# Splitting the second FFN product's matmuls into 256 columns, and another order of SBUF tiles

## The chip, the cores and the metric

The kernel runs on one NeuronCore of one Trainium2 chip. The metric is the device time of one execution in microseconds (us), from outside the program; the profile's span, from the first to the last instruction, is a few us shorter.

## The reference

Linear attention over 8 batches, 8 heads, 576 positions and a head dimension of 64, followed by a feed-forward network (FFN) on 4608 tokens of 512 values with 2048 hidden units, all in float32:

```python
q_s = softmax(q, axis=-1)
k_s = softmax(k, axis=2)
kv  = einsum('bhsd,bhse->bhde', k_s, v)
x   = einsum('bhsd,bhde->bhse', q_s, kv)     # 4608 tokens x 512 after reshaping
h   = x @ w_in                               # first FFN product, 512 -> 2048
g   = h * sigmoid(1.702 * h)
out = g @ w_out                              # second FFN product, 2048 -> 512
```

## The kernel before, in words

The 4608 tokens are taken in nine tiles of 512 (`t` from 0 to 8). For each tile the hidden units are taken in eight steps (`NS`) of two blocks of 128. All values of both products are split into a high and a low part of type float32r, and each product is the sum of three: high by high, high by low, low by high (the loop over `e`).

In tiles 0 and 1 the first product is `plain1` (L794): matmuls of 512 columns, stationary operand a tile `wj`, moving operand a tile `xp`. In tiles 2 to 8 it is `ffn1` (L841): seven smaller products in each step, from which the hidden values are added up on VectorE. Each of the seven is six matmuls of 256 columns; the stationary operand is a 128-column slice of `wj` or `wt` (two buffers of each kind, taken in turn by the step's parity), the moving operand half a row of a tile `xo`. So there are 7 x 8 x 7 = 392 such products, 2352 matmuls.

The second product is `ffn2` (L904), in all nine tiles: eight units in each step, each unit three matmuls of 512 columns into one of four PSUM banks. The stationary operand is a 128-column slice of `gh` or `gl` (the activation's high and low part), the moving operand a row of a tile `w` (half of the weight's high and low part). That is 9 x 8 x 8 = 576 units, 1728 matmuls. Every MATMUL of the program comes with a LDWEIGHTS of its own, also where two that follow each other have the same stationary operand.

Between these, for the next tile, the attention runs: products of k and v (L634), transposes of q (L683), and q times kv (L704).

The order of the work on every engine is made by the class `Plan` on the host, before anything runs: each operation is given an engine, a cost and a rank, and `Plan.forward` makes an order from them. The ranks of TensorE's operations lay L841's products and L904's units side by side through a step (L892 and L760).

The tiles in SBUF are allocated one behind the other by `sb`, in the order in which the program names them (L196 to L251, and later ones as they are first used). In one partition a tile of `gs`, `wj`, `xo` or `w` takes 4096 bytes, one of `wt` 8192, a `g`, `kt`, `qt`, `qT` or `tmp` 2048, all of them multiples of 512. Those that aren't: four `vt` and `vl` of 2080 bytes (4 x 512 + 32), two `qm` and `r` of 32, and `first` of 64 (L251), which stands behind all `wj`, `wide` and `wt0` and ahead of the tiles for `w`, `xp` and `xo`. `wt1` is first used, and so allocated, behind `first`; `gs` stands ahead of `vt`, `qm`, `r` and `vl`. Slices begin at multiples of 512 bytes of their tile. So where the operands of a matmul begin, modulo 512 bytes, follows from this order:

| line | stationary | moving | moving less stationary, modulo 512, before |
|---|---|---|---|
| L841 | `wj`, `wt0` | `xo` | 64 |
| L841 | `wt1` | `xo` | 0 |
| L794 | `wj` | `xp` | 64 |
| L904 | `gh`, `gl` | `w` | 4 x 32 + 32 + 2 x 32 + 32 + 64 = 320 |

Of the kernel before, what the change touches and what calls it, by code (L numbers as in the profile page):

```python
# [10 lines left out]
F32R = mybir.dt.float32r  # L11
# [125 lines left out]
def efficient_attention_then_gelu_ffn(  # L137
# [27 lines left out]
    nc = tc.nc  # L165
    B, H, S, D = q.shape
    NTOK, DM = out.shape
    FF = w_out.shape[0]
    P = 128
    C = 4  # L170
    TB = P * C
    HT = TB // 2
    NB = NTOK // TB
    NP = H // 2
# [4 lines left out]
    CM = SM // P  # L179
    ST = S - SM  # L180
    W = D + 1
# [9 lines left out]
    bank = [psum.tile([P, 512], F32, name=f"bank{i}") for i in range(8)]  # L191

    def sb(name, shape, dtype=F32, tag=None):
        return const.tile(shape, dtype, name=name, tag=tag or name)

    ident = sb("ident", [P, P])  # L196
    kvn = [sb(f"kvn{i}", [P, NP, D]) for i in range(2)]
    gt = [[sb(f"g{i}{u}", [P, 2, HT]) for i in range(2 - u)] for u in range(2)]
    gs = [[sb(f"g{s}{i}", [P, 2, 2, HT], F32R) for i in range(2)] for s in "hl"]
    tt = sb("tt", [P, 4, HT])  # L200
    tmp = [sb(f"tmp{i}", [P, DM]) for i in range(2)]
    kt = [sb(f"kt{i}", [P, 2, CM, D]) for i in range(NP)]
    vt = [sb(f"vt{i}", [P, 2, CM, W]) for i in range(NP)]
    qt = [sb(f"qt{i}", [P, C, 2, D]) for i in range(NP)]
    qT = [sb(f"qT{i}", [P, TB]) for i in range(2)]
    mx = [sb(f"mx{i}", [P, 2, D]) for i in range(NP)]
    m1 = sb("m1", [P, 2, 2, D])
    qm = [sb(f"qm{i}", [P, 2 * C]) for i in range(2)]
    r_ = sb("r", [P, 2, NP])
    rs = [r_[:, i] for i in range(2)]  # L210
    kl, vl = sb("kl", [P, H, D]), sb("vl", [P, H, W])
    wj = [[sb(f"wj{i}{jj}", [P, 2, KC, P], F32R) for jj in range(2)] for i in range(2)]
    wts = {}

# [4 lines left out]


    wide = sb("wide", [P, 4, DM], tag="wt0")
    kept = [[dram.tile([P, 2 * DM], F32, name=f"kept{p}{jj}") for jj in range(2)] for p in range(NS)]
    kept_t = [dram.tile([P, 4 * DM], F32, name=f"kept_t{p}") for p in range(NS)]

# [75 lines left out]
    def R(t, step, off=0.0):  # L300
        return SLOTS * (NS * t + step) + off
# [42 lines left out]
    def next_tmp(n):  # L344
        nt[n] += 1
        i = nt[n] % n
        return (tmp[i] if i < 2 else wide[:, i - 2]), ("tmp", i)
# [36 lines left out]
    def pair(t, step):  # L384


        return NS - 1 - step if t % 2 else step
# [501 lines left out]
    def ffn2(t, step):  # L889
        p, gi = pair(t, step), step % 2  # L890
        ov = out[t * TB : (t + 1) * TB, :].rearrange("(p c) m -> p c m", c=C)
        slots = iter((2, 2.3, 2.6, 6.3, 6.6, 10.3, 10.6, 13))  # L892
        units = [(c, jj) for jj in range(2) for c in range(C)] if t < 2 else [(c, jj) for c in (2, 3, 0, 1) for jj in range(2)]
        opened = set()
        for c, jj in units:
            u, cs = c // 2, slice(c % 2 * P, (c % 2 + 1) * P)
            first_, last = step == 0 and c not in opened, step == NS - 1 and c in opened
            opened.add(c)

            def run(c=c, jj=jj, u=u, cs=cs, first_=first_, last=last):  # L900
                gx, gl = (gs[e][gi][:, jj, u, cs] for e in range(2))
                wh, wl = wo[p, jj][:, 0], wo[p, jj][:, 1]
                for e, (l, r) in enumerate(((gx, wh), (gx, wl), (gl, wh))):
                    nc.tensor.matmul(bank[c], l, r, start=first_ and e == 0, stop=last and e == 2)  # L904

            rank = R(t, step + 1, next(slots))
            reads = (("gs", gi, 0, u, jj), ("gs", gi, 1, u, jj), f"wo{p}{jj}")
            plan.add("PE", 0.70, reads, (("bank", c),), rank, run)
            if not last:
                continue  # L910
            o, T = next_tmp(2)

            def run_o(c=c, o=o):
                (nc.vector.tensor_copy if c % 2 else nc.scalar.copy)(o, bank[c])

            def run_d(c=c, o=o):
                nc.sync.dma_start(out=ov[:, c, :], in_=o)

            plan.add("DVE" if c % 2 else "ACT", 0.65, (("bank", c),), (T,), rank - PRIOR, run_o)
            plan.add("SP", 0.4, (T,), (("out", t, c),), rank - PRIOR, run_d, size=P * DM * 4)  # L920
# [83 lines left out]
```

## Time and profile before

| | |
|---|---|
| time, median of 3 runs | 853.64 us (851.61 to 854.23) |
| span of the profiled execution | 850.0 us (no other time of it is shown) |
| TensorE busy | 840.8 us, 99% of the span |
| weight loads busy | 720.9 us, 85% |
| VectorE, ScalarE busy | 520.6 us (61%), 496.4 us (58%) |
| mean granted TensorE clock | 0.999 of full speed |

Matmuls are pipelined: the profile gives each a duration from its start to its modelled end, and the next one starts before that. So the busy time of a line is not the time that it costs; this is read from the timeline, as the distance of one group's start from the next one's. In the timeline, adjacent instructions of one line and the same tiles are one row: its start, its length from the first start to the last end, and how many they are.

### The profile page before, as it was taken

What the parts mean: (1) busy time and instruction counts of PE and PEld (TensorE: products, weight loads), DVE (VectorE), ACT (ScalarE), POOL (GpSimd) and SP (SyncE); (2) the same over time, 40 slices, a digit from 0 to 9 for tenths busy, and PEclk for the clock granted to TensorE, in tenths of its full rate; (3) what the DMA queues carried; (4) which work ended last, traced back from release to release, by engine and by line L of the source; (5) the groups of instructions that cost most, each with busy time, mean ns of one, the idle gap of its engine ahead of it and who ended that gap; (6) DMA issues with size and microseconds to landing.
All of it is one profiled execution on the core that took longest, in us unless ns stands there. A gap on an engine that the chain in (4) does not pass through costs nothing.

```text
span 850.0 us, 14608 instructions
## 1 busy us (share of the span) xinstructions
PE 840.8 (99%) x5644; PEld 720.9 (85%) x5644; DVE 520.6 (61%) x1082; ACT 496.4 (58%) x839; POOL 116.5 (14%) x175
## 2 busy tenths in 40 slices
PE   9999999999999999999999999999999999999998
PEld 4686788878898898889988999899988998899996
DVE  8899995989636884456645674475356533353333
ACT  4698879769636757446744766565366533343332
POOL 1000021120114131110211021100110011101110
PEclk9999999999999999999999999999999999999999
DMA  9999945894469738564765385623664165416541
GB/s 290 267 346 359 253 156 173 246 329 159 115 206 250 212 77 235 170 199 106 217 187 160 118 209 189 192 88 98 197 171 155 51 202 171 149 42 207 173 149 51
DMA packets 127845, 155.63 MB, mean 183 GB/s; under 512 B 76576, under 2 KB 105760, under 8 KB 121376
## 3 DMA queue, kind: packets, MB, share of 16 engines
q0 software_dynamic: 25248, 83.37, 32.3%
q1 hardware_dynamic: 102528, 71.32, 28.5%
q8 instruction: 45, 0.74, 0.4%
q14 instruction: 24, 0.20, 0.1%
HBM read 128.45 MB, written 26.21 MB: 182 GB/s over the span
## 4 chain that ended last, share of the span: by engine, by line
PE 93%; DVE 3%; DMA 2%; ACT 1%; issue 1%; DVEq 0%
PE bank L904 44%; PE bank L841 33%; PE bank L794 8%; PE bank L634 2%; PE bank L704 2%; DMA raw<-in_moe_w_out 2%; PE bank L683 2%; PE bank L296 1%; PE bank L582 0%; DVE wj L368 0%; PE bank L583 0%; DVE w L368 0%; DVE raw L337 0%; DVE kt L556 0%; DMA out<-tmp 0%
## 5 line engine op out<-in xcount | busy, mean ns | idle before, releaser
L904 PE MATMUL bank<-w,gh 128*128 128x512 f32 x1152 | 358.6, 392 | 0.3 <-DVE w L368 0.3
L904 PE MATMUL bank<-w,gl 128*128 128x512 f32 x576 | 226.4, 393 | 0.0
L904 PEld LDWEIGHTS bank<-w,gh 128*128 128x128 f32 x1152 | 199.9, 188 | 30.5 <-DVE w L368 1.1
L841 PE MATMUL bank<-xo,wt 128*128 128x256 f32 x1344 | 188.8, 281 | 0.0
L841 PEld LDWEIGHTS bank<-xo,wt 128*128 128x128 f32 x1344 | 177.4, 188 | 11.1 <-DVE g L854 0.8
L841 PEld LDWEIGHTS bank<-xo,wj 128*128 128x128 f32 x1008 | 136.0, 188 | 12.3 <-issue 1.6
L841 PE MATMUL bank<-xo,wj 128*128 128x256 f32 x1008 | 144.6, 279 | 0.5 <-ACT tt L865 0.5
L857 ACT ACTIVATE g<-g 128x512 f32<-128x512 f32 x112 | 58.8, 525 | 143.7 <-DVE g L854 143.1
L904 PEld LDWEIGHTS bank<-w,gl 128*128 128x128 f32 x576 | 108.3, 188 | 23.3
L854 DVE TENSOR_TENSOR g<-bank,tt 128x256 f32<-128x256 f32 x168 | 70.8, 422 | 88.7 <-PE bank L841 88.4
L885 DVE TENSOR_TENSOR gl<-g,gh 128x512 fp32r<-128x512 f32 x112 | 77.3, 691 | 72.3 <-ACT gh L882 71.7
L854 DVE TENSOR_TENSOR tt<-bank,tt 128x256 f32<-128x256 f32 x112 | 47.3, 423 | 105.4 <-PE bank L841 88.2
L397 POOL DMA_DIRECT2D wj<-kept x96 | 59.6, 621 | 378.8 <-PE bank L841 320.2
L794 PE MATMUL bank<-xp,wj 128*128 128x512 f32 x384 | 100.7, 396 | 2.4 <-ACT g L809 1.5
L794 PEld LDWEIGHTS bank<-xp,wj 128*128 128x128 f32 x384 | 71.0, 188 | 21.9 <-issue 2.6
L882 ACT CAST gh<-g 128x512 fp32r<-128x512 f32 x112 | 69.5, 621 | 3.2
L857 ACT ACTIVATE g<-bank 128x256 f32<-128x256 f32 x56 | 21.7, 387 | 73.0 <-PE bank L841 72.8
L545 POOL PARTITION_ALL_REDUCE mx<-mx x32 | 34.6, 1082 | 198.8 <-DVE mx L541 198.7
L397 POOL DMA_DIRECT2D wt<-kept_t x42 | 22.4, 532 | 125.0 <-PE bank L841 125.0
L857 ACT ACT_TABLE_LOAD x27 | 34.6, 1283 | 0.5
L664 ACT ACT_TABLE_LOAD x26 | 33.4, 1283 | 0.5
L865 ACT COPY tt<-bank 128x256 f32<-128x256 f32 x56 | 20.8, 371 | 18.3 <-PE bank L841 18.0
(103 smaller groups left out, 794.9 us busy)
## 6 DMA issues: line engine op xcount, KB each, us to landing
wt<-kept_t POOLq DMA_DIRECT2D x42, 1024.0 KB, 5.3
wj<-kept POOLq DMA_DIRECT2D x54, 512.0 KB, 3.7
wj<-kept POOLq DMA_DIRECT2D x42, 256.0 KB, 4.8
out<-tmp SPq DMA_DIRECT2D x36, 256.0 KB, 3.1
kt<-in_k SPq DMA_DIRECT2D x32, 256.0 KB, 4.5
raw<-in_moe_w_in SPq DMA_DIRECT2D x16, 512.0 KB, 8.5
raw<-in_moe_w_out SPq DMA_DIRECT2D x16, 512.0 KB, 7.4
kept<-wj SPq DMA_DIRECT2D x16, 512.0 KB, 6.9
```

Of the source, the lines that this page charges most:

```text
L397: "POOL", 1.0, (key,), (ring,), R(t, step - 2, off), lambda: nc.gpsimd.dma_start(out=out(), in_=src), size=size
L545: nc.gpsimd.partition_all_reduce(flat, flat, P, bass_isa.ReduceOp.max)
L634: nc.tensor.matmul(pk[r0 : r0 + D, m, cols], lhs, rhs, start=c == 0, stop=c == CM, tile_position=(0, r0))
L664: nc.scalar.activation(x, x, AF.Exp)
L794: nc.tensor.matmul(bank[bk], w[:, l, c, :], x[:, r], start=c == 0 and e == 0, stop=c == KC - 1 and e == 2)
L841: nc.tensor.matmul(ph[bk], w, x[:, r, c, :], start=opens and c == 0 and e == 0, stop=c == 1 and e == 2, skip_group_check=True,)
L854: return lambda: nc.vector.tensor_tensor(out=o, in0=ph[bk], in1=x, op=ALU.add)
L857: return lambda: nc.scalar.activation(o, x, AF.Gelu_apprx_sigmoid)
L865: vec("ACT", act(n), (ZB,), (A,), 2, lambda: nc.scalar.copy(a, ph[Z]))
L882: vec("ACT", act(2 * n), half, H, slot, lambda c=c, gh=gh: nc.scalar.copy(gh, c))
L885: nc.vector.tensor_tensor(out=gl, in0=c, in1=gh.bitcast(F32), op=ALU.subtract)
L904: nc.tensor.matmul(bank[c], l, r, start=first_ and e == 0, stop=last and e == 2)
```

## The change

Each matmul of L904 becomes two (L908 in the new file), one for each half of the 512 columns, with the same stationary operand. And the tiles are named in another order: `vt`, `qm`, `r` and `vl` come ahead of `gs`, and `wt1` is allocated at once behind `wide`, ahead of `first`.

```diff
     kvn = [sb(f"kvn{i}", [P, NP, D]) for i in range(2)]
+    vt = [sb(f"vt{i}", [P, 2, CM, W]) for i in range(NP)]
+    qm = [sb(f"qm{i}", [P, 2 * C]) for i in range(2)]
+    r_ = sb("r", [P, 2, NP])
+    rs = [r_[:, i] for i in range(2)]
+    vl = sb("vl", [P, H, W])
+    gs = [[sb(f"g{s}{i}", [P, 2, 2, HT], F32R) for i in range(2)] for s in "hl"]
     gt = [[sb(f"g{i}{u}", [P, 2, HT]) for i in range(2 - u)] for u in range(2)]
-    gs = [[sb(f"g{s}{i}", [P, 2, 2, HT], F32R) for i in range(2)] for s in "hl"]
...
-    vt = [sb(f"vt{i}", [P, 2, CM, W]) for i in range(NP)]
...
-    qm = [sb(f"qm{i}", [P, 2 * C]) for i in range(2)]
-    r_ = sb("r", [P, 2, NP])
-    rs = [r_[:, i] for i in range(2)]
-    kl, vl = sb("kl", [P, H, D]), sb("vl", [P, H, W])
+    kl = sb("kl", [P, H, D])
...
     wide = sb("wide", [P, 4, DM], tag="wt0")
+    wts[1] = sb("wt1", [P, 2, 4, 2 * P], F32R, tag="wt1")
...
                 for e, (l, r) in enumerate(((gx, wh), (gx, wl), (gl, wh))):
-                    nc.tensor.matmul(bank[c], l, r, start=first_ and e == 0, stop=last and e == 2)
+                    for h in range(2):
+                        cols = slice(h * HT, (h + 1) * HT)
+                        nc.tensor.matmul(
+                            bank[c][:, cols], l, r[:, cols], start=first_ and e == h == 0,
+                            stop=last and e == 2 and h == 1, skip_group_check=True,
+                        )
```

What is left between the stationary and the moving operand's tiles is `first` alone: 64 bytes modulo 512 for L904, and for every product of L841, those with `wt1` among them.

TensorE, a step of a tile from 2 on (`gh`, `gl` with `w` is the second product, `xo` with `wt` or `wj` the first; `ident` with `qt` is a transpose of q), before:

```order
L841 MATMUL bank_68<-xo_2032,wt_1534 128x256 x6
L683 MATMUL bank_69<-ident,qt_94 128x128 x4
L841 MATMUL bank_67<-xo_2046,wt_1534 128x256 x6
L904 MATMUL bank_63<-w,gh_78 128x512 x2
L904 MATMUL bank_63<-w,gl_80 128x512
L904 MATMUL bank_64<-w,gh_78 128x512 x2
L904 MATMUL bank_64<-w,gl_80 128x512
L841 MATMUL bank_68<-xo_2065,wj_109 128x256 x6
```

and now:

```order
L843 MATMUL bank_68<-xo_2386,wt_1765 128x256 x6
L685 MATMUL bank_69<-ident,qt_98 128x128 x4
L843 MATMUL bank_67<-xo_2406,wt_1765 128x256 x6
L908 MATMUL bank_63<-w,gh_83 128x256 x4
L908 MATMUL bank_63<-w,gl_85 128x256 x2
L908 MATMUL bank_64<-w,gh_83 128x256 x4
L908 MATMUL bank_64<-w,gl_85 128x256 x2
L843 MATMUL bank_68<-xo_2428,wj_109 128x256 x6
```

Nothing changes places; the second product's matmuls are twice as many and half as wide, and from tile 2 on no matmul of 512 columns is left in a step but for those of the attention.

TensorE, a step of tile 0 (`xp` with `wj` is the first product there), before:

```order
L904 MATMUL bank_65<-w,gh_77 128x512 x2
L904 MATMUL bank_65<-w,gl_79 128x512
L794 MATMUL bank_68<-xp_458,wj_111 128x512 x3
L904 MATMUL bank_66<-w,gh_77 128x512 x2
L904 MATMUL bank_66<-w,gl_79 128x512
L794 MATMUL bank_68<-xp_464,wj_111 128x512 x3
```

and now:

```order
L908 MATMUL bank_65<-w,gh_82 128x256 x4
L908 MATMUL bank_65<-w,gl_84 128x256 x2
L796 MATMUL bank_68<-xp_459,wj_111 128x512 x3
L908 MATMUL bank_66<-w,gh_82 128x256 x4
L908 MATMUL bank_66<-w,gl_84 128x256 x2
L796 MATMUL bank_68<-xp_465,wj_111 128x512 x3
```

Here too the places are the same, and the first product keeps its 512 columns. On VectorE, ScalarE, GpSimd and SyncE every instruction stands where it stood.

## Rows read from the trace of the kernel before

**Rows 1.** The page: busy time by engine, granted clock by slice, the chain by line.

```profile
PE 840.8 (99%) x5644; PEld 720.9 (85%) x5644; DVE 520.6 (61%) x1082; ACT 496.4 (58%) x839; POOL 116.5 (14%) x175
...
PEclk9999999999999999999999999999999999999999
...
PE bank L904 44%; PE bank L841 33%; PE bank L794 8%; PE bank L634 2%; PE bank L704 2%; DMA raw<-in_moe_w_out 2%; PE bank L683 2%; PE bank L296 1%; PE bank L582 0%; DVE wj L368 0%; PE bank L583 0%; DVE w L368 0%; DVE raw L337 0%; DVE kt L556 0%; DMA out<-tmp 0%
```

**Rows 2.** Groups of instructions by line, whole span: busy us, mean ns, idle before.

```profile
L904 PE MATMUL bank<-w,gh 128*128 128x512 f32 x1152 | 358.6, 392 | 0.3 <-DVE w L368 0.3
L904 PE MATMUL bank<-w,gl 128*128 128x512 f32 x576 | 226.4, 393 | 0.0
L904 PEld LDWEIGHTS bank<-w,gh 128*128 128x128 f32 x1152 | 199.9, 188 | 30.5 <-DVE w L368 1.1
L841 PE MATMUL bank<-xo,wt 128*128 128x256 f32 x1344 | 188.8, 281 | 0.0
L841 PEld LDWEIGHTS bank<-xo,wt 128*128 128x128 f32 x1344 | 177.4, 188 | 11.1 <-DVE g L854 0.8 <-DVE mx L540 0.5 <-issue 0.5
```

**Rows 3.** Timeline of PE, 503 to 513.5 us: start, length, line, tiles, count.

```profile
503.54 0.60 PE L683 MATMUL bank<-ident,qt 128*128 128x128 f32 x4
503.89 0.95 PE L841 MATMUL bank<-xo,wj 128*128 128x256 f32 x6
504.68 0.63 PE L904 MATMUL bank<-w,gh 128*128 128x512 f32 x2
...
506.75 0.84 PE L841 MATMUL bank<-xo,wj 128*128 128x256 f32 x6
507.43 0.84 PE L841 MATMUL bank<-xo,wt 128*128 128x256 f32 x6
508.11 0.62 PE L904 MATMUL bank<-w,gh 128*128 128x512 f32 x2
...
508.80 0.62 PE L904 MATMUL bank<-w,gh 128*128 128x512 f32 x2
...
509.49 1.52 PE L841 MATMUL bank<-xo,wt 128*128 128x256 f32 x12
```

**Rows 4.** Timeline of PE, 513.5 to 525 us, where `wt` is `wt1`.

```profile
514.30 0.87 PE L841 MATMUL bank<-xo,wj 128*128 128x256 f32 x6
515.01 0.63 PE L904 MATMUL bank<-w,gh 128*128 128x512 f32 x2
...
517.77 0.87 PE L841 MATMUL bank<-xo,wj 128*128 128x256 f32 x6
518.48 0.89 PE L841 MATMUL bank<-xo,wt 128*128 128x256 f32 x6
...
520.59 1.60 PE L841 MATMUL bank<-xo,wt 128*128 128x256 f32 x12
522.03 0.63 PE L904 MATMUL bank<-w,gh 128*128 128x512 f32 x2
...
522.73 0.84 PE L841 MATMUL bank<-xo,wj 128*128 128x256 f32 x6
523.41 0.62 PE L904 MATMUL bank<-w,gh 128*128 128x512 f32 x2
```

**Rows 5.** Timeline of PE, 345.9 to 349 us: a product behind L704.

```profile
345.62 0.61 PE L704 MATMUL bank<-qT,kvn 64*64 64x256 f32 x8
346.16 0.95 PE L841 MATMUL bank<-xo,wj 128*128 128x256 f32 x6
346.95 0.62 PE L904 MATMUL bank<-w,gh 128*128 128x512 f32 x2
```

**Rows 6.** Timeline of PE, 728 to 735 us: products behind the last L704.

```profile
728.29 1.09 PE L704 MATMUL bank<-qT,kvn 64*64 64x512 f32 x8
729.31 0.98 PE L841 MATMUL bank<-xo,wj 128*128 128x256 f32 x6
730.12 0.87 PE L841 MATMUL bank<-xo,wt 128*128 128x256 f32 x6
730.83 0.63 PE L904 MATMUL bank<-w,gh 128*128 128x512 f32 x2
```

## The prediction

> **What bounds the kernel now.** I read the page first. TensorE is busy for 99% of the span, the others for 61% at most, the granted clock stands at its upper level, 2.4 GHz, in all forty slices, and of the chain that ended last 44% lies on L904 and 33% on L841 [rows 1]. TensorE waits for nearly nothing: ahead of these lines' matmuls stand 0.3 us of idle time, and ahead of their loads some 30 us that lie under running matmuls [rows 2]. So only the distance from one matmul's start to the next one's counts. The groups by line don't tell it: they give durations that overlap (392 ns for 512 columns, 281 for 256) [rows 2]. The timeline does: a group's start less the one before it.
>
> I count in **blocks** of 1536 columns: one product of L841 (six matmuls of 256) or one unit of L904 (three of 512). Both have to stream the same columns, so by columns alone a block would cost the same in each. It doesn't:
>
> - **Tight**, L841 at 64 bytes apart: 506.75, 507.43, 508.11, 0.68 us each, a row of length 0.84; a row of two blocks 1.52 [rows 3].
> - **Loose**, the same shape at the same 64 bytes: 514.30 to 515.01 and 517.77 to 518.48, 0.71 us each, length 0.87 [rows 4].
> - `wt1`, 0 bytes apart: 520.59 to 522.03, two blocks in 1.44 us, 0.72 each [rows 4].
> - L904, 512 columns, 320 bytes apart: 508.11, 508.80, 509.49, 0.69 each [rows 3]; four units from 515.01 to 517.77, 2.76 us, 0.69 each [rows 4].
>
> Means over all such starts from 226 us to the end, without those around a stop, give the third digit: 0.680 tight, 0.707 loose, 0.718 for `wt1`, 0.689 for L904. Of the 280 products of L841 at 64 bytes 169 are tight and 111 loose; none of the 112 with `wt1` is tight. The timeline's lengths sort them: 0.84 and 1.52 against 0.86 to 0.89 and 1.58 to 1.60, and 0.95 to 0.98 where the first matmul pays a stop.
>
> **What decides between tight and loose** is the point of this change, since afterwards both products run on matmuls of 256 columns at 64 bytes. Three things are to be seen.
>
> 1. A product right behind other work starts loose. Behind the transposes at 503.54 the product costs 0.79 (0.95 long: the stop and then loose ones) [rows 3]; behind the L704 of 728.29 it is 0.98 long and the next product, 0.71, still loose [rows 6]. Of 20 products at 64 bytes right behind L683, L704 or L634, 19 are loose. One is tight: 0.95 long behind an L704, with the six in 0.79 though its stop was longer than that behind transposes [rows 5].
> 2. The pace holds as long as only such products follow. In all 72 places where two or three products at 64 bytes stand right behind one another the second has the pace of the first, as at 506.75 and 507.43 [rows 3] and at 729.31 and 730.12 [rows 6].
> 3. What ends the loose pace are the 512-column units of L904, and now and then `wt1`: loose at 503.89, three units from 504.68 on, tight at 506.75 [rows 3]; loose `wt1` at 520.59, two units, tight at 522.73 [rows 4]. Not always: 514.30 loose, four units, 517.77 loose again [rows 4].
>
> My reading: with 256 columns a weight load is due in each matmul's time, and a load that is a little late stays late; a matmul of 512 has the slack to catch up. The change takes these matmuls out of tiles 2 to 8.
>
> **A rule against the rows.** The rows show one shape at one address distance at two speeds, and a third at 0 bytes [rows 3, 4]. The Trainium skill, in TensorE: Matmul & The Clock Gate, section "Step-by-step: what each phase is for", says that TensorE has two independent read ports and that "Loading the next tile's weights doesn't steal SBUF read bandwidth from the running matmul"; by that the new order of tiles would be worth nothing, part 4 below would be 0 and the sum 1.2 higher. The trace disagrees: 0.718 against 0.680 for the same columns.
>
> **The change, part by part**, in us of the profiled span.
>
> 1. L904 in tiles 2 to 8: 7 x 8 x 8 = 448 units, now six matmuls of 256. If loose 448 x (0.707 - 0.689) = +8.1; if tight 448 x (0.680 - 0.689) = -4.0. I take loose, by points 1 and 2.
> 2. L841's tight products, 169, lose what made them tight: 169 x 0.027 = +4.6; if the pace is tight, 0.
> 3. L841's loose products at 64 bytes, 111: 0; if tight -111 x 0.027 = -3.0.
> 4. `wt1`, from 0 to 64 bytes, 112 products: 112 x (0.707 - 0.718) = -1.2; if tight 112 x (0.680 - 0.718) = -4.3.
> 5. L904 in tiles 0 and 1, 128 units: between 128 x -0.009 = -1.2 and 128 x 0.018 = +2.3. There L794 keeps its 512 columns between the units and can end the loose pace. I take 0.
> 6. One restart in 20 was tight, and such a stretch then stays so until the next stop. I take 8% of the 840 blocks of parts 1 to 4 as tight: 840 x 0.08 x -0.027 = -1.8.
> 7. The 1728 further weight loads of 188 ns [rows 2] cost nothing by themselves: they lie under the matmul ahead of them, as L841 shows, which loads for every 256 columns already and is tight at that. If this cover is thin, it shows as the loose pace, which is priced.
> 8. The moved tiles cost the other engines nothing: no instruction of theirs moves, and they are idle for 39% or more [rows 1]. Nothing waits longer on TensorE, and none of its operations changes places.
>
> Sum: 8.1 + 4.6 - 1.2 + 0 - 1.8 = **+9.7 us**, a span of 859.7. The median of the runs, 853.64, stands 3.6 above the span of the profiled execution, so I predict **863.3 us**. All loose, with tiles 0 and 1: 8.1 + 4.6 - 1.2 + 2.3 = +13.8, 867.4.
>
> **The rivals.**
>
> *The tight pace holds.* Nothing disturbs the alignment that L841 has when it is tight: a stretch that once got into 0.680 stays there, as in the 50 pairs of tight products, and if the restarts land tight the whole of both products runs at it. Sum: -4.0 + 0 - 3.0 - 4.3 - 1.2 = -12.5, 841.1 us. For it: one tight restart exists [rows 5], what decides there is a few ns, and the tiles of q and of its transposes move as well. Against it: 19 of 20. The point from which it decides: about half of the blocks tight, where 11.5 us of loss in parts 1 to 4 become a gain of 11.3. Chance 0.20.
>
> *The mixture stays.* Some other event resets the pace as the 512 columns did, say a weight load that waits for its semaphore, and six in ten blocks are tight as now: a block costs 0.6 x 0.680 + 0.4 x 0.707 = 0.691, so L904 +0.9, `wt1` 112 x -0.027 = -3.0, together -2.1, 851.5 us. For it: the loads of L841 often carry waits. Against it: such waits stand in the 72 places of point 2 too, and none changed the pace there. Chance 0.10.
>
> *A constant for each matmul, and no effect of addresses.* Then a split costs 1728 times that constant. The rows speak against any cost at all: two tight matmuls of 256 take less than one of 512 (0.680 against 0.689 for the block) [rows 3]. Chance 0.03. By the Trainium skill's section "Back-to-back issue gap" of TensorE: Matmul & The Clock Gate the distance is N/2.4 + 2.5 ns; an estimate from that is 1728 x 2.5 ns = +4.3 us, 857.9.
>
> *The change doesn't do what it says*: the order of TensorE shows the split, and the sizes of the tiles give the 64 bytes; I give this no chance of its own.
>
> **How the numbers follow.** A measurement of this kernel tells a difference of about 0.3%, 2.6 us, from none. The loose pace (forecast) has 0.67, spread from 857 to 867 by how many restarts land tight; with the constant per matmul 0.70 are slower. The mixture, 0.10, lies within 0.3%. The tight pace, 0.20, is faster. The likeliest case's own range is 857 to 868. The range that should hold 8 in 10 takes in the mixture and half-tight outcomes at its lower end, and leaves out the clearly tight case: 849 to 868.
>
> **What would show it.** Right: in the timeline from 226 us on, rows of L843 at 0.87 and of L908 (six matmuls: x4 and x2) about 0.71 apart, from one stop to the next, whole stretches at one pace; the stretch from the last L704 to the end (121 us before) longer by 2 us or more; no more idle time ahead of the matmuls. Wrong: rows of 0.84 through whole stretches (the tight rival), or changes from 0.87 to 0.84 within a stretch that has only matmuls of 256 columns (the mixture). Steps 4 and 7 are wrong if products with `wt1` stay at 0.72, or if blocks of either line cost more than 0.72.

## The result, and the profile after

| | before | after |
|---|---|---|
| time, median of 5 runs each | 852.35 us (850.90 to 854.23) | 863.89 us (862.76 to 866.31) |
| span of the profiled execution | 850.0 us | 860.9 us |
| TensorE busy | 840.8 us | 852.9 us |
| weight loads busy | 720.9 us | 807.4 us |
| ratio after to before | | 1.0143, 95% interval 1.0126 to 1.0161 |

The changed kernel is slower by 11.5 us. The page after, with its busy time, the granted clock and the chain by line, where [rows 1] stood:

```profile
PE 852.9 (99%) x7372; PEld 807.4 (94%) x7372; DVE 522.1 (61%) x1082; ACT 496.9 (58%) x839; POOL 116.2 (14%) x175
...
PEclk9999999999999999999999999999999999999999
...
PE bank L908 45%; PE bank L843 32%; PE bank L796 8%; DMA raw<-in_moe_w_out 3%; PE bank L636 2%; PE bank L706 2%; PE bank L685 2%; PE bank L298 1%; PE bank L584 0%; PE bank L585 0%; DVE w L370 0%; DMA out<-tmp 0%; DVE wide L335 0%; DVE wj L370 0%; DVE raw L339 0%
```

TensorE still is the bound, busy for the same share, at the same granted clock, with 1728 more matmuls. The other engines' busy times are those of before within 1.5 us. The groups by line, where [rows 2] stood:

```profile
L908 PE MATMUL bank<-w,gh 128*128 128x256 f32 x2304 | 364.6, 279 | 0.5 <-DVE w L370 0.4
L908 PE MATMUL bank<-w,gl 128*128 128x256 f32 x1152 | 227.9, 279 | 0.0
L908 PEld LDWEIGHTS bank<-w,gh 128*128 128x128 f32 x2304 | 315.0, 188 | 6.2 <-DVE w L370 0.9
```

No new idle time ahead of the matmuls (0.5 us against 0.3), and loads of the same 188 ns. The idle time ahead of the loads that belong to `gh` fell from 30.5 us to 6.2, with a load for every 256 columns now. So again the distance of the starts has to say it. The timeline of PE after, around the same transposes as in [rows 3]:

```profile
507.49 0.60 PE L685 MATMUL bank<-ident,qt 128*128 128x128 f32 x4
507.84 0.95 PE L843 MATMUL bank<-xo,wj 128*128 128x256 f32 x6
508.63 0.63 PE L908 MATMUL bank<-w,gh 128*128 128x256 f32 x4
...
509.34 0.63 PE L908 MATMUL bank<-w,gh 128*128 128x256 f32 x4
...
510.05 0.63 PE L908 MATMUL bank<-w,gh 128*128 128x256 f32 x4
...
510.75 0.87 PE L843 MATMUL bank<-xo,wj 128*128 128x256 f32 x6
511.46 0.87 PE L843 MATMUL bank<-xo,wt 128*128 128x256 f32 x6
512.16 0.63 PE L908 MATMUL bank<-w,gh 128*128 128x256 f32 x4
```

From 508.63 on every block, of either line, takes 0.70 to 0.71 us. Before, the same products had come down to 0.68 at 506.75 [rows 3]. Here nothing brings them down: from this stop to the next one 209 matmuls follow, all loose. A stop, here and below, is a place where TensorE does other work (L636, L685, L706 in this file). Of the 39 stops from 226 us on one has tight blocks behind it, the same as in [rows 5]:

```profile
346.88 1.09 PE L706 MATMUL bank<-qT,kvn 64*64 64x256 f32 x16
347.91 0.95 PE L843 MATMUL bank<-xo,wj 128*128 128x256 f32 x6
348.70 0.62 PE L908 MATMUL bank<-w,gh 128*128 128x256 f32 x4
...
349.38 0.62 PE L908 MATMUL bank<-w,gh 128*128 128x256 f32 x4
```

0.68 a block, through 142 matmuls, to the next stop. This stretch also shows what the split would give if its pace held: L908's units at 0.68, where L904 had 0.69. One more stretch from 226 us on is tight, 160 matmuls of tile 2, behind a pause at 228 us in which TensorE does no other work: one distance there is 193 ns, some 75 ns longer than its neighbours. Together these are 6% of the 256-column matmuls from 226 us on. Ahead of that, tile 2's first blocks, behind 512-column matmuls of L796, are tight until 225 us.

In what follows "tight" is a distance of 113.3 ns between two starts (0.680 us a block) and "loose" one of 117.8 (0.707), from the starts of the timeline from 226 us on, without those at stops.

### The profile page after: what moved, and what is told of

Its sections match the earlier page's. It is cut to its first block, busy times and chain, and to the rows that moved or that the text cites. A ratio compares the mean times of both kernels' runs of the same rounds, so it can differ in the third digit from the quotient of the medians.

```text
span 860.9 us, 18064 instructions
## 1 busy us (share of the span) xinstructions
PE 852.9 (99%) x7372; PEld 807.4 (94%) x7372; DVE 522.1 (61%) x1082; ACT 496.9 (58%) x839; POOL 116.2 (14%) x175
## 4 chain that ended last, share of the span: by engine, by line
PE 93%; DMA 3%; DVE 2%; ACT 1%; issue 0%; DVEq 0%; ACTq 0%
PE bank L908 45%; PE bank L843 32%; PE bank L796 8%; DMA raw<-in_moe_w_out 3%; PE bank L636 2%; PE bank L706 2%; PE bank L685 2%; PE bank L298 1%; PE bank L584 0%; PE bank L585 0%; DVE w L370 0%; DMA out<-tmp 0%; DVE wide L335 0%; DVE wj L370 0%; DVE raw L339 0%
## 5 line engine op out<-in xcount | busy, mean ns | idle before, releaser
L908 PE MATMUL bank<-w,gh 128*128 128x256 f32 x2304 | 364.6, 279 | 0.5 <-DVE w L370 0.4
L908 PEld LDWEIGHTS bank<-w,gh 128*128 128x128 f32 x2304 | 315.0, 188 | 6.2 <-DVE w L370 0.9
L908 PE MATMUL bank<-w,gl 128*128 128x256 f32 x1152 | 227.9, 279 | 0.0
L843 PE MATMUL bank<-xo,wt 128*128 128x256 f32 x1344 | 189.1, 281 | 0.0
L908 PEld LDWEIGHTS bank<-w,gl 128*128 128x128 f32 x1152 | 175.6, 187 | 0.0
L843 PEld LDWEIGHTS bank<-xo,wt 128*128 128x128 f32 x1344 | 170.5, 188 | 2.1 <-issue 1.3
L843 PE MATMUL bank<-xo,wj 128*128 128x256 f32 x1008 | 146.6, 280 | 0.5 <-ACT tt L867 0.5
L843 PEld LDWEIGHTS bank<-xo,wj 128*128 128x128 f32 x1008 | 130.1, 188 | 3.2 <-issue 1.6
L796 PE MATMUL bank<-xp,wj 128*128 128x512 f32 x384 | 101.0, 397 | 0.9 <-ACT g L811 0.6
L796 PEld LDWEIGHTS bank<-xp,wj 128*128 128x128 f32 x384 | 67.4, 188 | 16.4 <-issue 2.6
```

What stands on the lines that cost most here:

```text
L796: nc.tensor.matmul(bank[bk], w[:, l, c, :], x[:, r], start=c == 0 and e == 0, stop=c == KC - 1 and e == 2)
L843: nc.tensor.matmul(ph[bk], w, x[:, r, c, :], start=opens and c == 0 and e == 0, stop=c == 1 and e == 2, skip_group_check=True,)
L908: nc.tensor.matmul(bank[c][:, cols], l, r[:, cols], start=first_ and e == h == 0, stop=last and e == 2 and h == 1, skip_group_check=True,)
```

## The experiments

Theory: between stops the pace of 256-column matmuls holds, and the change took away what ended the loose one. Rival A: the new order of tiles is what costs. Rival B: a fixed price for each further matmul and load.

### 1. The split alone

```diff
-                    nc.tensor.matmul(bank[c], l, r, start=first_ and e == 0, stop=last and e == 2)
+                    for h in range(2):
+                        cols = slice(h * HT, (h + 1) * HT)
+                        nc.tensor.matmul(bank[c][:, cols], l, r[:, cols], ...)
```

> The split with the old order of tiles: L904 becomes matmuls of 256 columns at 320 bytes apart, wt1 stays at 0. Theory (the pace of 256-column matmuls is set at a stop and held, and only the 512-column units ended the loose pace): the products at 64 bytes stay at 0.707 us a block from stop to stop, L904 has 0.707 or more, so +8 to +14 us on the time before, 860 to 868 us. Rival A (the new order of tiles is what costs, the split is harmless): within 0.3% of before, 850 to 856. Rival B (a fixed price for each of the 1728 further matmuls with its load, some 6 ns): +10 to +12, 862 to 865, but then L843's products keep their share of 0.680 blocks.

Measured: 854.56 us, ratio 1.0034 (1.0020 to 1.0048). A miss of my range: the split alone costs a quarter of the whole. Its timeline behind an L634, L906 being the second product at 320 bytes:

```profile
294.01 0.74 PE L906 MATMUL bank<-w,gh 128*128 128x256 f32 x4
...
295.54 0.63 PE L906 MATMUL bank<-w,gh 128*128 128x256 f32 x4
...
296.24 0.87 PE L841 MATMUL bank<-xo,wj 128*128 128x256 f32 x6
296.95 0.87 PE L841 MATMUL bank<-xo,wt 128*128 128x256 f32 x6
```

So 320 bytes has the loose pace, 0.70 to 0.71, and here it holds across both distances. But over the run 66% of L906's matmuls and 45% of L841's are tight, against 6% with the whole change. Something in this kernel still ends the loose pace. Rival B is out: 1728 further matmuls cost 2.5 us, 1.5 ns each, not 6.

### 2. The new order of tiles alone

L904 whole, 512 columns at 64 bytes; all else as in the changed kernel (the split's six lines are taken back).

> The new order of tiles with L904 whole, 512 columns at 64 bytes. Theory: the 512-column units still end the loose pace, L904 has 0.689 a block as L794 has at 64 bytes, wt1 goes from 0.718 to a mixture of 0.680 and 0.707: 0 to 4 us below the time before, 848 to 853. Rival A: above before, 860 or more, with L904 blocks over 0.70. Rival B: 849 to 853 too.

Measured: 850.55 us, ratio 0.9988 (0.9972 to 1.0004); no difference that this measurement can tell. Rival A is out too: neither part costs what both cost together. The timeline, first behind one transpose, then behind another:

```profile
503.65 0.95 PE L843 MATMUL bank<-xo,wj 128*128 128x256 f32 x6
504.45 0.63 PE L906 MATMUL bank<-w,gh 128*128 128x512 f32 x2
...
506.52 0.87 PE L843 MATMUL bank<-xo,wj 128*128 128x256 f32 x6
507.23 0.87 PE L843 MATMUL bank<-xo,wt 128*128 128x256 f32 x6
...
528.57 0.95 PE L843 MATMUL bank<-xo,wt 128*128 128x256 f32 x6
529.37 0.63 PE L906 MATMUL bank<-w,gh 128*128 128x512 f32 x2
...
530.75 1.52 PE L843 MATMUL bank<-xo,wt 128*128 128x256 f32 x12
```

Three units of 512 columns leave the first stretch loose (0.87), two turn the second tight (1.52 for two). So the wide matmuls end the loose pace in some stretches and not in others. 57% of L843's matmuls are tight here.

### 3. What a wider matmul has to be

```diff
+    def widths(t, step, c, jj, e):
+        at = 256
+        if t > 1 and (c, jj) == (2, 0):
+            at = {2: (512, 512, 256), 3: (288, 256, 256), 4: (272, 256, 256), 5: (320, 256, 256), 6: (384, 256, 256), 7: (512, 256, 256), 8: (512, 512, 512)}[t][e]
+        return [(a, z) for a, z in ((0, at), (at, 512)) if z > a]
```

> The changed kernel, in which one L908 unit of each step in tiles 2 to 8 is cut another way, to see what ends the loose pace: widths of its three products 512, 512, 256+256 in tile 2; 288+224 for the first in tile 3; 272+240 in tile 4; 320+192 in tile 5; 384+128 in tile 6; 512 for the first alone in tile 7; three whole 512 in tile 8. Theory, in the reading that a late load stays late until a wider matmul gives it slack: behind a unit with any of the wide ones the blocks go from 0.707 to 0.680 and stay, up to 24 us in all, 840 to 850 us. Theory, in the reading that the phase of the two streams decides and a wider matmul only shifts it: some widths do it, others not or only at every second or third time, 845 to 865 us. Rival B: 863, all blocks at 0.707 as in the changed kernel.

Measured: 861.90 us, one run. The first cut of tile 2, the first of tile 4, and that of tile 8:

```profile
241.66 0.87 PE L843 MATMUL bank<-xo,wj 128*128 128x256 f32 x6
242.37 0.62 PE L914 MATMUL bank<-w,gh 128*128 128x512 f32 x2
...
244.42 0.84 PE L843 MATMUL bank<-xo,wj 128*128 128x256 f32 x6
...
418.31 0.63 PE L914 MATMUL bank<-w,gh 128*128 128x272 f32 x4
...
419.02 0.63 PE L914 MATMUL bank<-w,gh 128*128 128x256 f32 x4
419.73 0.63 PE L914 MATMUL bank<-w,gh 128*128 128x256 f32 x4
...
779.17 0.87 PE L843 MATMUL bank<-xo,wj 128*128 128x256 f32 x6
779.88 0.63 PE L914 MATMUL bank<-w,gh 128*128 128x512 f32 x2
...
781.94 0.84 PE L843 MATMUL bank<-xo,wj 128*128 128x256 f32 x6
```

One matmul of 272, 288, 320, 384 or 512 columns never ended the loose pace. Two whole ones did it when their two distances were 229 and 232 ns (three times), and not when they were 235 and 232 (three times); from tight they led to loose (once). Three did it in tile 8 (235, 232, 231 ns), and in each later step led from tight to tight (226, 229, 232). The reading of the late load that catches up falls by tile 7: behind a single matmul of 512 columns, 233 to 235 ns against the load's 188, the blocks stayed loose in all eight steps. The narrower cuts don't test it, as each wide matmul there is followed by one of 128 to 240 columns. From a tight pace three 512-column matmuls have the distances 226, 229, 232 ns; the figures above fit a cycle in which the place where they leave it decides the pace behind them. That is the second reading, and its range, 845 to 865, held.

### 4. Other distances

The changed kernel with other tiles behind `first`, so that all operands of both products lie 256 (`vt` and `qm`), 128 (`qm`), 192 (`vt`) or 96 (`r`) bytes apart. The edit for 256:

```diff
     first = sb("first", [P, 16])
+    vt = [sb(f"vt{i}", [P, 2, CM, W]) for i in range(NP)]
+    qm = [sb(f"qm{i}", [P, 2 * C]) for i in range(2)]
```

> The changed kernel with vt and qm behind first: all operands of both products 256 bytes apart instead of 64. Theory: the paces belong to the distance; no row shows 256 columns at 256 bytes, so a block may have 0.680 to 0.72, but one pace holds from stop to stop; 840 to 872 us. If addresses do nothing (Rival B, a fixed price for each matmul): 863 as the changed kernel, with blocks of 0.707.

> The changed kernel with qm behind first: all operands of both products 128 bytes apart. Theory (the distance sets which paces there are, and between stops one is held; 64 and 320 share theirs, 0.680 and 0.707, and 256 has 0.720): a held pace that isn't 0.720, and if 128 has only one and it is the tight one, 0.680 throughout: 839 to 842 us; if it has two as 64 has, 850 to 866; if it has only a loose one, 862 to 880. Rival (a late weight load stays late, wherever the operands lie): 863, blocks of 0.707.

> The changed kernel with vt behind first: all operands of both products 192 bytes apart. The same as for 128: 839 to 842 us if its only pace is 0.680, 850 to 866 if it has two, 862 to 880 if only a loose one. Rival: 863, blocks of 0.707.

> The changed kernel with r behind first: all operands of both products 96 bytes apart, between 64 and 128. If only whole steps of 64 bytes matter: the paces of 64 or of 128, nothing between. If single steps of 32 matter: a pace of its own, 0.68 to 0.72; 840 to 880 us. Rival: 863, blocks of 0.707.

| bytes apart | us, one run each (64: median of five) | mean distance, 256 columns |
|---|---|---|
| 64 (the change) | 863.89 | 117.5 ns |
| 96 | 878.18 | 120.0 ns |
| 128 | 872.87 | 118.6 ns |
| 192 | 853.69 | 115.0 ns |
| 256 | 878.17 | 119.9 ns |

At 256 bytes one pace, of 0.72 us, holds between all stops, as expected. The time lies above its range of 840 to 872: a miss. Of its 14 us over the change 3.2 arise ahead of the first L843 (at 222.1 us, in the change at 218.9). Three units in a row:

```profile
517.93 0.64 PE L908 MATMUL bank<-w,gh 128*128 128x256 f32 x4
...
518.64 0.64 PE L908 MATMUL bank<-w,gh 128*128 128x256 f32 x4
...
519.36 0.64 PE L908 MATMUL bank<-w,gh 128*128 128x256 f32 x4
```

The times at 96, 128 and 192 bytes lie in the ranges given for them. At 192 bytes 64% are tight, and behind an L636 the blocks come to the tight pace within three matmuls:

```profile
396.81 0.74 PE L908 MATMUL bank<-w,gh 128*128 128x256 f32 x4
...
397.62 0.62 PE L908 MATMUL bank<-w,gh 128*128 128x256 f32 x4
...
398.30 0.62 PE L908 MATMUL bank<-w,gh 128*128 128x256 f32 x4
```

So where the operands lie modulo 512 sets which paces there are, in steps of 32 or finer (96 is neither 64 nor 128). With the instructions the same, the four kernels and the change lie 24 us apart: Rival B's 863 for all of them is out a second time. None has the tight pace alone. One rival stands untested: in all kernels of this document `w`, `xp` and `xo` begin at the same place modulo 512, since the same tiles in all stand ahead of them, and only the stationary operand's tiles move. Whether the distance counts, or the stationary operand's own place, these runs don't tell; "bytes apart" names the kernels.

### 5. Whole units behind the stops

```diff
+                whole = stopped.pop() if stopped else (c, jj) == (2, 0)
...
+                    for a, z in ((0, 512),) if whole else ((0, HT), (HT, 512)):
```

with `stopped` set by each L638, L688 and L710.

> The changed kernel, at 64 bytes, in which the first L908 unit behind each stop (L636, L685, L706) and one unit in each step have three whole matmuls of 512 columns. Theory: such a unit takes a loose pace that the transposes left to 0.680 and keeps a tight one, as the last tile of the run with widths by tile shows (235, 232, 231 ns, then tight to the end; 226, 229, 232 from tight to tight); behind L706 it does so only for about half of the stops. 20% to 35% of the blocks of tiles 2 to 8 stay at 0.707: 844 to 852 us. If three whole ones did nothing outside the last tile: 860 to 864.

Measured: 857.79 us, ratio 1.0071 (1.0050 to 1.0092); 31% of L847's and 35% of L913's split matmuls tight. A miss: better than the change, worse than expected. Behind the transposes (L688) there are two kinds of loose. Where the first distance was 202 or 203 ns, the whole unit took 235, 232, 231 or so and tight blocks followed, in nine stops of nine; where it was 204 or 205, it took 233, 236, 229 or so and they stayed loose, in eight of nine. Where it was 201, once, they stayed loose too. So a nanosecond or two at the stop goes with one kind or the other. The stretch from the last stop to the end, 1006 matmuls long in the changed kernel, lies behind an L710; its whole units took 233, 236, 229 or so, and it stayed loose.

### 6. Which of the two breakers was missing

Two things in the kernel before could end a loose pace, and are called breakers here: the 512-column units of L904, and the products with `wt1` at 0 bytes. The changed kernel has neither. Now the changed kernel with `wt1` allocated late again (0 bytes), and the split with the old order but for `wt1` (64 bytes, `gs` at 320):

```diff
-    wts[1] = sb("wt1", [P, 2, 4, 2 * P], F32R, tag="wt1")
```

> The changed kernel without the line that allocates wt1 early: gs at 64 bytes and split, but the products with wt1 0 bytes apart as before. Theory (what the split alone still had, and the change lost, is a thing that changes the pace between stops: the wt1 products at 0 bytes): 852 to 858 us, tight and loose blocks mixed, changes of pace at wt1 products. Rival (gs at 64 instead of 320 bytes is what cost): 861 to 866, loose.

> The split with the old order but for wt1, which is allocated early: gs 320 bytes apart, wt1 64. Theory: no wt1 at 0 and no 512-column matmul is left, so the loose pace holds from stop to stop as in the changed kernel: 860 to 867 us. Rival: 852 to 856, as the split alone.

| | `gs` 320 | `gs` 64 |
|---|---|---|
| L904 split, `wt1` 0 | 854.56 (1.0034) | 855.40 (1.0051, 1.0034 to 1.0068) |
| L904 split, `wt1` 64 | 858.49 (1.0085, 1.0070 to 1.0100) | 863.89 (1.0143) |

With `wt1` at 0 the loss is mostly gone, at either place of `gs`. How it is done shows in the run with `wt1` at 0 and `gs` at 64:

```profile
301.99 0.87 PE L842 MATMUL bank<-xo,wj 128*128 128x256 f32 x6
302.70 0.63 PE L907 MATMUL bank<-w,gh 128*128 128x256 f32 x4
...
303.40 0.88 PE L842 MATMUL bank<-xo,wt 128*128 128x256 f32 x6
304.12 0.84 PE L842 MATMUL bank<-xo,wj 128*128 128x256 f32 x6
304.80 0.62 PE L907 MATMUL bank<-w,gh 128*128 128x256 f32 x4
...
307.52 0.88 PE L842 MATMUL bank<-xo,wt 128*128 128x256 f32 x6
308.24 0.62 PE L907 MATMUL bank<-w,gh 128*128 128x256 f32 x4
```

Loose to 303.40; then a product with `wt1` (0.88), and behind it tight. The next one with `wt1`, at 307.52, leaves the tight pace as it was. Counted over this run, away from stops: in 25 places `wt1` products came behind loose blocks, and in 16 of them tight blocks follow; in 48 they came behind tight blocks, and tight blocks follow in all. In the split alone it is 12 of 19, and 54 of 54. The products that cost most for themselves, 0.718 us a block, were what brought the others down.

The run with `gs` at 320 and `wt1` at 64 came out 1.5 us below its range. Its paces hold as expected, from stop to stop, but the stretch behind the last stop, a fifth of all, was tight:

```profile
736.06 1.09 PE L705 MATMUL bank<-qT,kvn 64*64 64x512 f32 x8
737.08 0.95 PE L842 MATMUL bank<-xo,wj 128*128 128x256 f32 x6
737.87 0.84 PE L842 MATMUL bank<-xo,wt 128*128 128x256 f32 x6
738.55 0.62 PE L907 MATMUL bank<-w,gh 128*128 128x256 f32 x4
```

1006 matmuls of 4.5 ns less are 4.5 us; with it loose the run would have been at 863, in the range. All four of its runs lie at 858.09 to 860.33, so that this stretch is probably tight in each, and not by a draw in one of them. Whether that comes from `gs` at 320 bytes or from something smaller at the stop, no run here tells.

### 7. 192 bytes and a whole unit in each step

The kernel at 192 bytes, its L908 unit (2, 0) of each step in tiles 2 to 8 left whole.

> All operands 192 bytes apart, every L908 unit split but one in each step of tiles 2 to 8, which stays three whole 512. At 192 bytes the split kernel had 63% of its blocks at 0.680 and took 852 to 854 us, with stretches of up to 532 matmuls at 0.707. Theory: the whole units end some of these stretches and keep the tight ones: 70% to 90% tight, 843 to 851 us. If whole units at 192 bytes shift a tight pace to a loose one: 853 to 860.

Measured: 854.25 us, ratio 1.0033 (1.0021 to 1.0044), half of the matmuls tight: a miss of the theory's range, and inside the other one. At 192 bytes a whole unit that meets a held pace turns it nearly each time: from tight (226, 236, 231 ns) to loose always, from loose (mostly 231, 229, 236) to tight with two exceptions. So it ends the loose stretches and as many tight ones.

### 8. The changed kernel once more

> The changed kernel once more, unaltered, for a second trace of it. Theory that the program decides the pace at each stop: the same stop as in its first trace, the L706 near 348 us, is followed by tight blocks, the other stops of tiles 2 to 8 by loose ones, 862 to 867 us. If the pace at a stop is drawn anew in each execution, about 1 stop in 20 is tight and another one: the long stretches decide, 855 to 867 us.

Measured: 864.15 us, span 862.1. The stop that was tight in the first trace:

```profile
348.45 0.98 PE L843 MATMUL bank<-xo,wj 128*128 128x256 f32 x6
349.26 0.63 PE L908 MATMUL bank<-w,gh 128*128 128x256 f32 x4
...
349.97 0.63 PE L908 MATMUL bank<-w,gh 128*128 128x256 f32 x4
```

Loose this time, 0.71 a block, as at every other stop from 226 us on: no 256-column matmul after 226 us is tight. So the program alone does not decide a stop; another execution can come out otherwise. (Whether both traces come from the same chip isn't known.) Only two stretches changed, the one behind the pause in tile 2 (160 matmuls, with a pause of the same 193 ns) and this one (142): 302 x 4.5 ns = 1.4 us, and the spans differ by 1.2.

## Why the prediction was right, point by point

What was forecast of the blocks was found: loose behind the stops, and held from one to the next. The reason given for it was wrong, and so was the weight of what ends the loose pace (both below). The time, 863.3 us, lies 0.6 below the measured; that close it is by luck, as it was built on the median of three runs before, 853.64, and the median of five is 852.35. The change forecast was +9.7 us, the change measured +11.5. In the profiled executions, with the distances of the starts summed over the same matmuls before and after:

| step | forecast | measured |
|---|---|---|
| 1, L904 of tiles 2 to 8 | +8.1 | 309.9 to 317.2: +7.3 |
| 2 to 4, L841 | +4.6 + 0 - 1.2 = +3.4 | 278.5 to 281.2: +2.7 |
| 5, tiles 0 and 1 | 0 (-1.2 to +2.3) | first L841 at 218.1, now at 218.9: +0.8 |
| 6, share of tight blocks | 8%, -1.8, in no line above | 6% from 226 us on, within the sums above |
| 7, 8, loads and other engines | 0 | 188 ns as before; busy times within 1.5 us |
| span | +9.7 | +10.9 |

- **Point 1**, a product behind a stop starts loose: held from 226 us on, at 38 of 39 stops, and at all 39 in the second trace. Tile 2's first blocks, behind L796, were tight in both.
- **Point 2**, the pace holds: held, for 209, 532 and 1006 matmuls where the longest row before had 18.
- **Point 3**, the 512-column units end the loose pace, `wt1` now and then: the weights were wrong. Either of the two saves most: without the wide matmuls but with `wt1` at 0 the loss is 0.34% to 0.51%, and with the wide matmuls but `wt1` at 64 there is none that can be told. Without both it is 0.85% (`gs` at 320) or 1.43% (the change). The prediction names the wide matmuls as what the change takes away; that the change takes away `wt1` at 0 bytes as well, which it priced as a gain, is why the forecast still came out. The split alone, by the same reasoning expected at 860 to 868, took 854.56.
- **The reading** (a late load stays late, a wide matmul has slack) was wrong: a single matmul of 512 columns changed nothing, in eight places of eight, and at 256 bytes every block costs 0.72 with the same loads. That the distances repeat in cycles fits a phase between two streams of reads, that of the loads and that of the moving operand; this is argued, and no run here shows what the phase is of in the chip.
- **Step 4** held for its own blocks: `wt1` at 64 bytes saved some 1.2 us of them (119.6 ns a matmul before, 117.8 where loose). What it left out is that this takes away a breaker, which is paid in steps 1 and 2.
- **The tight rival** failed where it was weak, at the stops. **The mixture** failed in the change, but is what the split alone and `wt1` at 0 show. **The constant price** gives 857.9, outside the measured runs (862.76 to 866.31). The split alone, at +2.5 us, lies below it too, and the paces of one kernel, 113.3 and 117.8 ns for the same matmuls, are not one price.

With nothing but addresses changed the split kernel takes from 853.69 us to 878.18. The Trainium skill's sentence on the independent read ports (TensorE: Matmul & The Clock Gate, "Step-by-step: what each phase is for") doesn't lead one to expect that: by it the next tile's load takes no read bandwidth from the running matmul. The traces don't bear it out for these matmuls, whose mean distances of 115.0 to 120.0 ns go with where the operands lie. That it is the load and the running matmul that hinder each other is the likeliest reading; it isn't shown by itself.

No kernel here beats the one before beyond its uncertainty; the order of tiles alone comes nearest, 0.9988 (0.9972 to 1.0004). What decides the kind of pace at a stop, a matter of one or two ns in the first distance, stays open. So does whether the distance counts or the stationary operand's own place, and whether any distance has the tight pace alone, as 32, 160, 224 and others weren't tried for both products.

## What to carry to other kernels

A price taken from a shape that runs at two paces belongs to a mixture, and the mixture to what breaks it up: before making everything like the best case, look in the timeline for what sets the best case going again, be it a wider matmul or a product that is itself dear. Distances of starts, and group lengths (0.84 and 0.87 us for six), tell such paces apart; a mean by line (281 ns for L841's matmuls with `wt` before and for L843's after) mixes them. And two changes that are each harmless can cost together, so measure them apart and together.

## What the runs showed of the hardware that was not expected

- Float32r matmuls of 256 columns with a load each have held paces that go with where their operands begin modulo 512: 113.3 and 117.8 ns at 64, 192 and 320 bytes apart, 120 at 256, repeating groups of distances from 115 to 122 ns at 128 and from 116 to 125 at 96 bytes. Only the stationary operand's place was moved.
- At 64 and 320 bytes a pace outlived 1006 matmuls, two tile buffers and four PSUM banks: loose in the change, tight with `gs` at 320. In these kernels it ended only at a stop or a pause, at matmuls of another width, or at products with another distance.
- At 64 bytes matmuls of 512 columns behind a tight pace had the distances 226, 229, 232 ns: three of them left it tight, seven times of seven in the last tile of the run with other widths, and two turned it loose, once. A single one behind a loose pace left it loose, eight times of eight.
- Behind the transposes the first distance went with the kind of loose pace: in the run with whole units 202 or 203 ns with the kind that they end, 204 or 205 with the one that they don't, at 17 stops of 18. At 201 ns, once, they didn't end it.
